# The first tiles' last decays taken out ahead of their flags, in an attention and two-expert-block kernel

## The chip, the core and the metric

The kernel runs on one core of a Trainium2 chip. The metric is the device time of one execution in microseconds (us), as the median of several runs. The kernel before takes 728.8 us (three runs: 727.46, 728.80 and 737.34).

## What is computed

Three stages follow each other on 3072 tokens of width 384 (4 sequences of 768 tokens, 8 heads of 48). The first is a linear attention with a decaying state, step by step:

```
for t in range(S):
    cur = einsum('bhd,bhe->bhde', u * k_t, v_t)
    y[t] = einsum('bhd,bhde->bhe', r_t, state + cur)
    state = w_t[..., None] * state + einsum('bhd,bhe->bhde', k_t, v_t)
```

The second sends each token to one of 8 experts (argmax of `x @ w_gate + bias`), computes `relu(x @ w1[e]) @ w2[e]` and scales by the softmax weight of that expert. The third is a dense block, `max(x @ v1, x @ v2, x @ v3) @ v_out`.

## The kernel before, in words

The attention works on 24 tiles of 128 tokens, 6 to a sequence, all heads at once. The rest of the kernel (experts and dense block, matmuls of 128x256 and 128x512) isn't touched. For each tile two blocks come from memory: `tq`, the transposed r, k and decay w (`load_t`, one DMA of 576 KB, into one of four buffers; tile 0's comes in three pieces, w first), and `nat`, the rows of v, r and k (`load_n`, 608 KB). All of these loads are issued by SyncE (SP), in the order of the program. Each load fills 96 of the 128 partitions of `tq`; the rest is padding, written once at the start by `pads(j)` for each buffer j (zeros for r and k, ones for w), and a load can't be issued before its buffer's padding is written.

What a tile goes through, by function, and on which engine:

- `flags(i)` (ScalarE): two passes over the tile's decays, 128x512, that sum how far they lie outside of allowed bounds into `flag`. Nothing reads `flag` before the plan for the experts (`check_w`).
- `cut_w(i)` (ScalarE): copies each head pair's last decay (128x4) into `wl`, and overwrites it in `tq` by a multiplication with `keep` (0 or 1 by partition). `flags` reads the decays whole, so it stands ahead of `cut_w`.
- `scan_f(i)` (VectorE): the running product of the decays into `prod`, by a scan over 128x512 that needs the cut decays; then a reciprocal, and `pt`, the product with `wl`.
- `mul_r`, `scan_r`, `mul_k` (VectorE): r times the product, the reverse scan, and k times it: `rt` and `kt`.
- `ktrans(i)`, `scores(i)` (TensorE): transposes of `kt`, copied to `kn` by ScalarE, and the 128x128 products of `kt` and `rt`, copied to `am` by ScalarE (two copies) and masked by GpSimd (POOL, `affine_select`).
- `kv(i)`, `output(i)` (TensorE): the tile's addition to the state, and the output into `yb` from `am`, v and the state `sbd`.
- `uterm_a(i)` (POOL), `usum(i)` (VectorE), `uterm_b(i)` (POOL): the term with u, from `nat`; `output_x(i)` (VectorE) adds it to `yb` and gives x, which `columns(i)` transposes (TensorE), ScalarE copies, and `logits_of` uses.

No scheduler decides the order: it is as written, and each engine runs its instructions strictly in that order. Tiles 0 and 1 stand in a prologue of their own; from then on the loop at `for i in range(NTILE - 2)` runs `scan_f` of tile i+2 together with the matmuls of tiles i and i+1, and `flags` and `cut_w` of tile i+3. `rows()` is a generator that puts some constants for the routing between the work of tiles 1 to 3: on VectorE a cast `mf`, which TensorE transposes (L172), and on POOL some twenty small memsets and iotas. `warm(n)` issues n matmuls of 128x512 on a tile of zeros, `wide`, whose result nobody reads; `WARM` lists how many stand at each of its places, and the fourth entry, for ordinary tiles of the loop, is 0.

Of the kernel before, what the change touches and what calls it, by code (L numbers as in the profile page):

```python
# [9 lines left out]
F32 = mybir.dt.float32  # L10
F32R = mybir.dt.float32r
BF16 = mybir.dt.bfloat16
I32 = mybir.dt.int32
U32 = mybir.dt.uint32
ACTF = mybir.ActivationFunctionType
# [6 lines left out]

W_LO, W_HI = 0.7, 1.4
P_LO = 1e-22
BIG = 1000000.0
OOB = 1 << 20
SLOT = object()
# [13 lines left out]


FIRST_GO = (9, 0, 0, 7, 8)
WARM = (16, 6, 4, 0, 3, 0)


@with_exitstack
def kernel(ctx: ExitStack, tc: tile.TileContext, rkw_t, v_t, vrk, u, modality, w_gate, bias, w1, w2, v1, v2,
# [56 lines left out]
    def ct(shape, dt, name):  # L105
        return const.tile(shape, dt, name=name)
# [18 lines left out]
    wg = ct([128, KD, E], F32, "wg")  # L125
    b0 = ct([128, 2, E], F32, "b0")
    brow = ct([128, NTILE, E], F32, "brow")
    flag = ct([128, NTILE, 2], F32, "flag")
    ctl = ct([128, 64], I32, "ctl")
    gctl = ct([128, 4], I32, "gctl")  # L130
    idxm = ct([128, NTILE], I32, "idxm")
# [541 lines left out]
    def attention(hooks):  # L673
        with ExitStack() as es:
# [26 lines left out]
            def v4(t):  # L701
                return t.rearrange("p (a c) -> p a c", a=HP)
# [6 lines left out]
            tq = [e1.tile([128, 3 * 512], F32, name=f"tq{j}") for j in range(NB)]  # L709
            keep = e1.tile([128, 1], F32, name="keep")  # L710
            DVE.memset(tq[0][96:128, 1024:1536], 1.0)
            DVE.memset(wide, 0.0)

            def r_of(i):
                return v4(tq[i % NB][:, 0:512])
# [4 lines left out]
            def w_of(i):  # L720
                return v4(tq[i % NB][:, 1024:1536])

            def pads(j, rk=POOL.memset, w=POOL.memset):
                rk(tq[j][:, 0:1024], 0.0)
                w(tq[j][:, 1024:1536], 1.0)

            def zeros(out, _):
                for q in range(2):
                    ACT.copy(out[:, q * 512:(q + 1) * 512], wide)
            POOL.memset(tq[0][96:128, 0:1024], 0.0)  # L730
            DVE.memset(tq[0][0:PAD, 1024:1536], 1.0)
            POOL.memset(neglo[:, 0:1], W_LO)
            POOL.memset(neglo[:, 1:2], -W_HI)
            POOL.memset(keep, 0.0)
            POOL.memset(keep[0:PAD], 1.0)
            POOL.memset(keep[96:128], 1.0)
            POOL.memset(keep[96:PAD + 2 * D], 0.0)
            DVE.memset(d1f, P_LO)
            DVE.memset(v4(d1f)[:, :, 0:1], 1.0)
            DVE.memset(d1r, 0.0)  # L740
            POOL.memset(tq[0][0:PAD, 0:1024], 0.0)
            pads(1, zeros)
            pads(2, DVE.memset, DVE.memset)
            make_identity(nc, ident)
            for t in sbd:
                POOL.memset(t, 0.0)
            pads(3)

            T = [dict() for _ in range(NTILE)]

            def load_t(i, parts=(slice(0, 3),)):
                b, c = divmod(i, NC)
                for q in parts:
                    SP.dma_start(out=tq[i % NB][PAD:PAD + 2 * D, q.start * 512:q.stop * 512],
                                 in_=rkw_t[b, c, :, :, q].rearrange("o d q a t -> (o d) (q a t)"))

            def load_n(i):
                n = np_.tile([128, HN + 2 * DM], F32, tag="nat", name="nat")
                SP.dma_start(out=n, in_=vrk[i * 128:(i + 1) * 128])
                T[i]["v"] = heads(n[:, 0:HN])[:, :, 0:D]  # L760
                T[i]["r"], T[i]["k"] = n[:, HN:HN + DM], n[:, HN + DM:HN + 2 * DM]
                T[i]["uv"] = n[:, HN:HN + DM]
# [19 lines left out]
            def flags(i):  # L782
# [4 lines left out]
                ACT.activation(out=jk, in_=wr, func=ACTF.Relu, scale=1.0, bias=neglo[:, 1:2],  # L787
                               accum_out=flag[:, i, 1:2])

            def cut_w(i):  # L790


                last = w_of(i)[:, :, 127:128]
                s = T[i]
                s["wl"] = a2.tile([128, HP, 1], F32, tag="wl", name="wl")
                ACT.copy(s["wl"], last)
                ACT.activation(out=last, in_=last, func=ACTF.Copy, scale=keep)

            def scan_f(i):

                s = T[i]
                f = tq[i % NB]
                DVE.tensor_tensor_scan(out=prod, data0=f[:, 1023:1535], data1=d1f, initial=0.0, op0=ALU.mult, op1=ALU.max)  # L803
                end = v4(prod)[:, :, 127:128]
                s["pt"] = a3.tile([128, HP, 1], F32, tag="pt", name="pt")
                DVE.reciprocal(v4(d1r)[:, :, 126:127], end)
                DVE.tensor_tensor(out=s["pt"], in0=end, in1=s["wl"], op=ALU.mult)

            def mul_r(i):
                s = T[i]  # L810
# [119 lines left out]
            loads, rows = constants_rest(pes)  # L930
            load_t(0, [slice(q, q + 1) for q in (2, 0, 1)])
            load_t(1)
            load_n(0)
            load_u()
            load_t(2)
            load_n(1)
            loads()
            SP.dma_start(out=wg, in_=w_gate.rearrange("(k p) e -> p k e", p=128))
            load_n(2)
            warm(WARM[0])  # L940
            flags(0)
            for i in range(2):
                cut_w(i)
                scan_f(i)
                mul_r(i)
                scan_r(i)
                mul_k(i)
                if i == 0:
                    flags(1)
                    ktrans(0)  # L950
                    scores(0)
                    warm(WARM[1])
                uterm_a(i)
            load_t(3)
            load_t(4)
            flags(2)
            cut_w(2)
            for i in range(NTILE - 2):
                n = i + 2
                if i + 5 < NTILE:  # L960
# [9 lines left out]
                    output_x(i - 1)  # L970
                ktrans(i + 1)
                scores(i + 1)
                if i:
                    columns(i - 1)
                uterm_a(n)
# [13 lines left out]
                state_b(i)  # L989
                slot()  # L990
                slot()
                for j in (0, 1) if i == 0 else (i + 1,):
                    usum(j)
                    uterm_b(j)
                slot()
# [621 lines left out]
```

## Time and profile before

| | |
|---|---|
| median of three runs | 728.8 us |
| the profiled execution | 736.0 us, span from first to last instruction 734.2 us |
| mean granted TensorE clock, share of 2.4 GHz | 0.973 |
| TensorE matmuls busy | 698.3 us, 95% of the span |
| VectorE busy | 468.8 us, 64% |
| ScalarE busy | 321.8 us, 44% |
| POOL busy | 327.6 us, 45% |

The attention fills the first quarter of the span, the experts and the dense block the rest. The shares are means over stages that differ: in the start, which the change is about, the engines wait for each other and for loads, and the clock that was granted to TensorE falls to half of 2.4 GHz and comes back. In a timeline row the first number is the start, the second the time during which the row's instructions ran (an "x2" row merges two); what stands in brackets is how long the engine had been idle just before, and what ended that.

### The profile page before, as it was taken

To read this page: it belongs to the slowest core of one execution; us is meant where nothing else is said; L and a number is where in the kernel's file an instruction comes from. 1 tells how busy PE (TensorE), PEld (TensorE's weight loads), DVE (VectorE), ACT (ScalarE), POOL (GpSimd) and SP (SyncE) were. 2 spreads that over 40 slices of the span, in tenths; PEclk is the share of its full clock that TensorE was granted. 3 is DMA by queue.
4 is the path that set the end of the run, shared out by engine and by line. 5 is a ranking of instruction groups with operands and counts; after the bars stand their busy time and mean duration, and the time that the engine had idled before them with its cause. 6 is when DMAs were issued, how large, how long until landed. Compare 5 with 4: busy or idle time off the path is not lost.

```text
span 734.2 us, 13120 instructions
## 1 busy us (share of the span) xinstructions
PE 698.3 (95%) x4948; PEld 636.8 (87%) x4956; DVE 468.8 (64%) x858; ACT 321.8 (44%) x695; POOL 327.6 (45%) x386
## 2 busy tenths in 40 slices
PE   5999999998799999999999999999999999999996
PEld 2788878897799899999999987988988989889886
DVE  5888988888387988889897979524234143142330
ACT  5576757674213656666666633221212212112111
POOL 5676669697546767777674435010200201101002
PEclk9799999998799989999999999999999999999999
DMA  8877769961023222222254232020200200000001
GB/s 239 224 224 218 230 179 246 283 219 35 1 75 109 66 87 66 65 83 71 66 164 151 87 130 87 1 86 1 76 11 1 89 0 12 33 0 33 12 0 48
DMA packets 28509, 69.86 MB, mean 95 GB/s; under 512 B 5173, under 2 KB 15189, under 8 KB 28436
## 3 DMA queue, kind: packets, MB, share of 16 engines
q1 hardware_dynamic: 23636, 59.43, 27.5%
q0 software_dynamic: 4800, 9.49, 4.1%
q8 instruction: 41, 0.67, 0.4%
q14 instruction: 32, 0.26, 0.1%
HBM read 83.24 MB, written 14.38 MB: 133 GB/s over the span
## 4 chain that ended last, share of the span: by engine, by line
PE 39%; issue 36%; DVE 11%; POOL 6%; ACT 4%; DMA 2%; another core or an unknown queue 1%; POOLq 0%; SPq 0%; DVEq 0%; ACTq 0%
PE mm L1226 9%; PE mm L1227 9%; PE mm L1225 9%; POOL out_dram L1310 3%; PE yb L867 3%; PE mm L833 2%; DMA nat<-in_vrk_dram 2%; PE lgps L222 1%; DVE prod L803 1%; PE yb L873 1%; PE lgps L855 1%; PE tp L846 1%; PE tp L1214 1%; ACT am L836 1%
## 5 line engine op out<-in xcount | busy, mean ns | idle before, releaser
L1290 DVE TENSOR_TENSOR w2r<-mm,w2r 128x512 f32<-128x512 f32 x72 | 49.7, 690 | 145.7 <-PE mm L1227 145.6
L1310 POOL DMA_INDIRECT out_dram<-w2r,oi_all x24 | 26.0, 1083 | 244.9 <-ACT w2r L1309 244.3
L1225 PE MATMUL mm<-w1h,vh 128*128 128x512 f32 x324 | 126.3, 390 | 1.5 <-DVE w2r L1290 1.5
L1226 PE MATMUL mm<-w1l,vh 128*128 128x512 f32 x324 | 126.2, 389 | 0.0
L1227 PE MATMUL mm<-w1h,vl 128*128 128x512 f32 x324 | 126.1, 389 | 0.0
L1226 PE MATMUL mm<-hl,w2h 128*128 128x256 f32 x312 | 91.0, 292 | 3.3 <-DVE hl L1239 3.3
L1225 PE MATMUL mm<-hh,w2h 128*128 128x256 f32 x312 | 91.7, 294 | 1.5 <-issue 1.5
L1227 PE MATMUL mm<-hh,w2l 128*128 128x256 f32 x312 | 90.7, 291 | 0.0
L1225 PE MATMUL mm<-xh,w1h 128*128 128x256 f32 x306 | 87.7, 287 | 0.0
L1227 PE MATMUL mm<-xh,w1l 128*128 128x256 f32 x306 | 87.4, 286 | 0.0
L1226 PE MATMUL mm<-xl,w1h 128*128 128x256 f32 x306 | 87.4, 286 | 0.0
L1292 ACT CAST w2h<-w2r 128x512 fp32r<-128x512 f32 x36 | 22.4, 622 | 135.8 <-DVE w2r L1290 135.8
L1225 PEld LDWEIGHTS mm<-w1h,vh 128*128 128x128 f32 x324 | 60.8, 188 | 14.9 <-DVE w2r L1290 2.4
L1227 PEld LDWEIGHTS mm<-w1h,vl 128*128 128x128 f32 x324 | 60.8, 188 | 12.7
L1226 PEld LDWEIGHTS mm<-w1l,vh 128*128 128x128 f32 x324 | 60.8, 188 | 12.4
L580 POOL TENSOR_TENSOR w2l<-w2r,w2h 128x384 fp32r<-128x384 f32 x44 | 50.8, 1158 | 37.9 <-ACT w2h L578 33.3
L1226 PEld LDWEIGHTS mm<-hl,w2h 128*128 128x128 f32 x312 | 62.3, 200 | 4.4 <-DVE hl L1239 4.0
L1225 PEld LDWEIGHTS mm<-hh,w2h 128*128 128x128 f32 x312 | 62.4, 200 | 1.8 <-issue 1.8
L1227 PEld LDWEIGHTS mm<-hh,w2l 128*128 128x128 f32 x312 | 62.2, 199 | 0.0
L1225 PEld LDWEIGHTS mm<-xh,w1h 128*128 128x128 f32 x306 | 59.6, 195 | 0.0
L1226 PEld LDWEIGHTS mm<-xl,w1h 128*128 128x128 f32 x306 | 59.6, 195 | 0.0
L1227 PEld LDWEIGHTS mm<-xh,w1l 128*128 128x128 f32 x306 | 59.6, 195 | 0.0
(294 smaller groups left out, 1614.9 us busy)
## 6 DMA issues: line engine op xcount, KB each, us to landing
w1r<-in_moe_w_dram SPq DMA_DIRECT2D x10, 1536.0 KB
w2r<-in_moe_w_dram SPq DMA_DIRECT2D x10, 1536.0 KB
nat<-in_vrk_dram SPq DMA_DIRECT2D x24, 608.0 KB
tq<-in_rkw_t_dram SPq DMA_DIRECT2D x23, 576.0 KB
stg<-in_moe_w_dram SPq DMA_DIRECT2D x18, 384.0 KB
x2t<-raw SPq DMA_DIRECT2D x12, 384.0 KB
w1r<-x2t SPq DMA_DIRECT2D x12, 384.0 KB
xs<-x SPq DMA_DIRECT2D x23, 192.0 KB
```

Of the source, the lines that this page charges most:

```text
L222: PE.matmul(logits[:, t, :], lhsT=xT[:, kk, :], rhs=wg[:, kk, :], start=(kk == 0), stop=(kk == KD - 1))
L580: eng.tensor_tensor(out=lo, in0=src, in1=hi.bitcast(F32), op=ALU.subtract)
L803: DVE.tensor_tensor_scan(out=prod, data0=f[:, 1023:1535], data1=d1f, initial=0.0, op0=ALU.mult, op1=ALU.max)
L833: PE.matmul(ps[o][:, p * 128:(p + 1) * 128], lhsT=s["kt"][q, p, :], rhs=s["rt"][q, p, :], start=True, stop=True)
L836: ACT.copy(am[:, 4 * o:4 * o + 4, :], ps[o].rearrange("p (h t) -> p h t", h=4))
L867: PE.matmul(yb[:, h * DV:(h + 1) * DV], lhsT=s["am"][:, 4 * (h % 2) + h // 2, :], rhs=s["v"][:, h, :], start=(h == 0), stop=(first and h = ...
L1225: PE.matmul(oc, lhsT=wh[:, kk, sl], rhs=xh[:, kk, :], start=first and kk == 0, stop=False)
L1226: PE.matmul(oc, lhsT=wh[:, kk, sl], rhs=xl[:, kk, :], start=False, stop=False)
L1227: PE.matmul(oc, lhsT=wl[:, kk, sl], rhs=xh[:, kk, :], start=False, stop=last and kk == nk - 1)
L1290: DVE.tensor_tensor(out=hv, in0=o, in1=hv, op=ALU.max)
L1292: ACT.copy(self.h2h[:, c, :], hv)
L1310: ins = POOL.indirect_dma_start(out=out[:, :], out_offset=bass.IndirectOffsetOnAxis(ap=ids[q][:, 0:1], axis=0), in_=ob, in_offset=None, bo ...
```

## The change

1. In the prologue and for tile 2, `cut_w` comes first and a new function `flags_behind` takes the place of `flags` behind it: it flags 127 of 128 decays of each head pair in `tq`, and the last one from `wl`, so four passes instead of two. `flag` gets three more columns for it.
2. The prologue no longer has `ktrans(0)` and `scores(0)` between tiles 0 and 1: they follow both tiles' `mul_k`. `cut_w(2)` follows them, and `flags_behind(2)` and `uterm_a(1)` move into the loop behind `scores(1)`. `usum(1)` and `uterm_b(1)` move from the loop's first pass into its second.
3. The padding of buffer 1 is written by VectorE (r, k) and POOL (w) right at the start, that of buffer 2 by ScalarE (r, k) and POOL (w); buffer 3's comes ahead of the memsets of `sbd`. `wide` is zeroed behind buffer 1's padding.
4. SP loads `tq` of tile 2 ahead of `nat` of tile 0, and `tq` of tile 3 ahead of `nat` of tile 2.
5. The prologue's `warm` calls have 20 and 4 matmuls instead of 16 and 6.
6. `pt` is computed with a lower bound of 1e-10 on `wl`, by one `scalar_tensor_tensor` instead of a `tensor_tensor`.

```diff
+WL_LO = 1e-10
-WARM = (16, 6, 4, 0, 3, 0)
+WARM = (20, 4, 4, 0, 3, 0)
-    flag = ct([128, NTILE, 2], F32, "flag")
+    FIRST = 3
+    flag = ct([128, NTILE + FIRST, 2], F32, "flag")
...
             DVE.memset(tq[0][96:128, 1024:1536], 1.0)
-            DVE.memset(wide, 0.0)
+            POOL.memset(tq[0][96:128, 0:1024], 0.0)
...
-            POOL.memset(tq[0][96:128, 0:1024], 0.0)
+            pads(1, DVE.memset)
+            DVE.memset(wide, 0.0)
             DVE.memset(tq[0][0:PAD, 1024:1536], 1.0)
+            POOL.memset(tq[0][0:PAD, 0:1024], 0.0)
+            DVE.memset(d1f, P_LO)
+            DVE.memset(v4(d1f)[:, :, 0:1], 1.0)
+            DVE.memset(d1r, 0.0)
             POOL.memset(neglo[:, 0:1], W_LO)
...
-            DVE.memset(d1f, P_LO)
-            DVE.memset(v4(d1f)[:, :, 0:1], 1.0)
-            DVE.memset(d1r, 0.0)
-            POOL.memset(tq[0][0:PAD, 0:1024], 0.0)
-            pads(1, zeros)
-            pads(2, DVE.memset, DVE.memset)
+            pads(2, zeros)
             make_identity(nc, ident)
+            pads(3)
             for t in sbd:
                 POOL.memset(t, 0.0)
-            pads(3)
...
+            def flags_behind(i):
+                jk = a1.tile([128, 512], BF16, tag="jk", name="jk")
+                for q, sign in enumerate((-1.0, 1.0)):
+                    ACT.activation(out=v4(jk)[:, :, 0:127], in_=w_of(i)[:, :, 0:127], func=ACTF.Relu, scale=sign,
+                                   bias=neglo[:, q:q + 1], accum_out=flag[:, i, q:q + 1])
+                    ACT.activation(out=v4(jk)[:, :, 127], in_=T[i]["wl"][:, :, 0], func=ACTF.Relu, scale=sign,
+                                   bias=neglo[:, q:q + 1], accum_out=flag[:, NTILE + i, q:q + 1])
...
-                DVE.tensor_tensor(out=s["pt"], in0=end, in1=s["wl"], op=ALU.mult)
+                DVE.scalar_tensor_tensor(out=s["pt"], in0=s["wl"], scalar=WL_LO, in1=end, op0=ALU.max, op1=ALU.mult)
...
             load_t(1)
+            load_t(2)
             load_n(0)
             load_u()
-            load_t(2)
             load_n(1)
+            load_t(3)
             loads()
...
             warm(WARM[0])
-            flags(0)
             for i in range(2):
                 cut_w(i)
                 scan_f(i)
+                flags_behind(i)
                 mul_r(i)
                 scan_r(i)
                 mul_k(i)
-                if i == 0:
-                    flags(1)
-                    ktrans(0)
-                    scores(0)
-                    warm(WARM[1])
-                uterm_a(i)
-            load_t(3)
+            ktrans(0)
+            scores(0)
+            uterm_a(0)
+            warm(WARM[1])
+            cut_w(2)
             load_t(4)
-            flags(2)
-            cut_w(2)
             for i in range(NTILE - 2):
...
                 scores(i + 1)
+                if i == 0:
+                    flags_behind(2)
+                    uterm_a(1)
...
-                for j in (0, 1) if i == 0 else (i + 1,):
+                for j in ((0,), (1, 2))[i] if i < 2 else (i + 1,):
                     usum(j)
                     uterm_b(j)
```

How the order on the engines changes is shown at three places. The first is ScalarE's prologue, before (`jk` is a pass of `flags`, `wl` and the write into `tq` are `cut_w`, `kn` and `am` the copies of tile 0's matmuls):

```order
L785 ACTIVATE jk_228,flag_89<-tq0_160,neglo_110 128x512
L787 ACTIVATE jk_228,flag_89<-tq0_160,neglo_110 128x512
L796 COPY wl_231<-tq0_160 128x4
L797 ACTIVATE tq0_160<-tq0_160,keep_164 128x4
L785 ACTIVATE jk_244,flag_89<-tq1_161,neglo_110 128x512
L787 ACTIVATE jk_244,flag_89<-tq1_161,neglo_110 128x512
L848 COPY kn_252<-tp_247 128x512
L836 COPY am_254<-mm_255 128x512
L836 COPY am_254<-mm_256 128x512
L796 COPY wl_278<-tq1_161 128x4
L797 ACTIVATE tq1_161<-tq1_161,keep_164 128x4
```

Tile 1's cut stood behind the copies of tile 0's transposes and scores. In the changed kernel the same place reads:

```order
L807 COPY wl_233<-tq0_160 128x4
L808 ACTIVATE tq0_160<-tq0_160,keep_164 128x4
L796 ACTIVATE jk_240,flag_89<-tq0_160,neglo_110 128x4x127
L798 ACTIVATE jk_240,flag_89<-wl_233,neglo_110 128x4
L796 ACTIVATE jk_240,flag_89<-tq0_160,neglo_110 128x4x127
L798 ACTIVATE jk_240,flag_89<-wl_233,neglo_110 128x4
L807 COPY wl_251<-tq1_161 128x4
L808 ACTIVATE tq1_161<-tq1_161,keep_164 128x4
L796 ACTIVATE jk_258,flag_89<-tq1_161,neglo_110 128x4x127
```

Each tile's cut stands ahead of its flags, and tile 1's has moved ahead of every copy from TensorE. The second place is ScalarE at tile 3, in the loop's first pass, in the changed kernel (before, the four rows of `flags_behind(2)`, `jk_339`, were not there, and the rest stood in the same order):

```order
L847 COPY am_324<-mm_326 128x512
L796 ACTIVATE jk_339,flag_89<-tq2_162,neglo_110 128x4x127
L798 ACTIVATE jk_339,flag_89<-wl_298,neglo_110 128x4
L796 ACTIVATE jk_339,flag_89<-tq2_162,neglo_110 128x4x127
L798 ACTIVATE jk_339,flag_89<-wl_298,neglo_110 128x4
L787 ACTIVATE jk_365,flag_89<-tq3_163,neglo_110 128x512
L789 ACTIVATE jk_365,flag_89<-tq3_163,neglo_110 128x512
L807 COPY wl_368<-tq3_163 128x4
L808 ACTIVATE tq3_163<-tq3_163,keep_164 128x4
```

Tile 2's flags now stand between tile 1's `am` copies and tile 3's cut. The third place is POOL in the loop's first two passes; `nat` with `u_b` is `uterm_a`, `nat` with `sh` is `uterm_b`, and nat_200, 204, 209 are tiles 0, 1, 2. Before:

```order
L770 TENSOR_TENSOR nat_209<-nat_209,u_b_156 128x384
L771 TENSOR_TENSOR nat_209<-nat_209 128x384
L780 TENSOR_TENSOR nat_200<-nat_200,sh_368 128x384
L780 TENSOR_TENSOR nat_204<-nat_204,sh_371 128x384
L166 MEMSET zt_390 128x384
L174 MEMSET on_394 128x128
L837 AFFINE_SELECT am_408<-am_408 128x512 x2
```

In the changed kernel tile 1's `uterm_b` (nat_204 with `sh_485`) comes behind the second pass's masks, tile 3's `uterm_a` and the routing constants, the last of which are the first three rows here:

```order
L203 MEMSET oe_105 128x4
L206 MEMSET d0c3_83 128x32
L207 MEMSET d0c3_83 128x8
L782 TENSOR_TENSOR nat_204<-nat_204,sh_485 128x384
L782 TENSOR_TENSOR nat_210<-nat_210,sh_488 128x384
L206 MEMSET d0c8_84 128x72
```

It moved by one pass of the loop; tile 2's (nat_210) stayed where it was, right behind.

## Rows read from the trace of the kernel before

**Rows 1.** Busy time by stretch: TensorE, weights, VectorE, ScalarE, POOL; granted clock, DMA share, GB/s

```profile
6.00:28.00 22.00, 14.51 (x87) 10.01 (x85) 15.70 (x29) 10.30 (x30) 10.07 (x14) 0.71 1.01 270
11.90:15.30 3.40, 3.40 (x21) 2.08 (x21) 0.03 (x1) 2.09 (x6) 0.96 (x2) 0.50 1.03 270
15.30:18.70 3.40, 1.20 (x19) 0.65 (x17) 3.30 (x6) 1.79 (x6) 3.24 (x5) 1.00 1.05 304
18.70:28.90 10.20, 8.97 (x55) 7.27 (x56) 8.90 (x18) 4.17 (x11) 6.20 (x9) 0.50 0.94 237
```

**Rows 2.** Timeline of ScalarE in the prologue

```profile
4.43 0.72 ACT L785 ACTIVATE jk<-tq,neglo 128x512 bf16<-128x512 f32 x1 [1.16 <-POOL ident masks.py:199]
...
6.06 0.18 ACT L796 COPY wl<-tq 128x4 f32<-128x4 f32 x1
6.33 0.30 ACT L797 ACTIVATE tq<-tq,keep 128x4 f32<-128x4 f32 x1
9.38 0.72 ACT L785 ACTIVATE jk<-tq,neglo 128x512 bf16<-128x512 f32 x1 [2.75 <-DMA tq<-in_rkw_t_dram]
...
11.82 0.59 ACT L848 COPY kn<-tp 128x512 f32<-128x512 f32 x1 [0.78 <-PE tp L846]
13.68 1.07 ACT L836 COPY am<-mm 128x512 f32<-128x512 f32 x2 [1.27 <-PE mm L833]
```

**Rows 3.** Timeline of VectorE: memsets, the scans of tiles 0 to 5, one cast

```profile
3.88 0.91 DVE L724 MEMSET tq<- 128x1024 f32 x1 [0.20 <-issue]
4.85 0.48 DVE L725 MEMSET tq<- 128x512 f32 x1
6.72 1.23 DVE L803 TENSOR_TENSOR_SCAN prod<-tq,d1f 128x512 f32<-128x512 f32 x1 [1.38 <-ACT tq L797]
...
15.27 1.23 DVE L803 TENSOR_TENSOR_SCAN prod<-tq,d1f 128x512 f32<-128x512 f32 x1 [4.26 <-ACT tq L797]
...
19.66 1.23 DVE L803 TENSOR_TENSOR_SCAN prod<-tq,d1f 128x512 f32<-128x512 f32 x1
...
25.92 1.23 DVE L803 TENSOR_TENSOR_SCAN prod<-tq,d1f 128x512 f32<-128x512 f32 x1 [0.71 <-ACT tq L797]
...
27.33 0.29 DVE L164 CAST mf<-mi 24x128 f32<-24x128 int32 x1
...
34.64 1.23 DVE L803 TENSOR_TENSOR_SCAN prod<-tq,d1f 128x512 f32<-128x512 f32 x1 [1.60 <-ACT tq L797]
...
40.72 1.23 DVE L803 TENSOR_TENSOR_SCAN prod<-tq,d1f 128x512 f32<-128x512 f32 x1 [0.61 <-ACT tq L797]
```

**Rows 4.** Timeline of TensorE: first warm-up, transposes, outputs, scores of tile 2

```profile
1.94 5.16 PE L926 MATMUL tp<-wide 128*128 128x512 bf16 x16 [1.94 <-DVE wide L712]
11.16 0.63 PE L846 MATMUL tp<-ident,kt 128*128 128x128 f32 x4 [4.06 <-DVE kt L824]
...
22.74 3.65 PE L867 MATMUL yb<-nat,am 128*128 128x48 f32 x16
...
29.80 1.16 PE L833 MATMUL mm<-rt,kt 64*128 64x128 f32 x16
...
31.27 1.88 PE L867 MATMUL yb<-nat,am 128*128 128x48 f32 x16
```

**Rows 5.** DMA issues of the attention's blocks, size of each

```profile
nat<-in_vrk_dram SPq DMA_DIRECT2D x24, 608.0 KB
tq<-in_rkw_t_dram SPq DMA_DIRECT2D x23, 576.0 KB
```

**Rows 6.** Groups on VectorE, 85 to 260 us: busy us, mean ns

```profile
L807 DVE TENSOR_TENSOR pt<-prod,wl 128x4 f32<-128x4 f32 x12 | 1.8, 152 | 0.0
...
L447 DVE SCALAR_TENSOR_TENSOR gb<-gexp,pids 128x4 f32<-128x4 f32 x1 | 0.2, 152 | 0.0
```

**Rows 7.** Timeline of POOL, second pass of the loop

```profile
31.70 1.23 POOL L837 TENSOR_SCALAR_AFFINE_SELECT am<-am 128x512 f32<-128x512 f32 x2 [2.87 <-ACT am L836]
...
37.39 0.83 POOL L780 TENSOR_TENSOR nat<-nat,sh 128x384 f32<-128x384 f32 x1
```

## The prediction, made before the changed kernel ran

> **What bounds the kernel now.** I read the timelines of the four engines over the first 45 us beside each other, since nothing behind the attention is edited, then the windows for the granted clock and the DMA share. In the timelines the reader is to see what each `scan_f` waited for: it starts a tile's work on VectorE, and its starts are the ruler of this prediction. They stand at 6.72, 15.27, 19.66, 25.92, 34.64 and 40.72 us for tiles 0 to 5 [rows 3]. Only tile 2's follows its predecessor at once, after 4.39 us, which is VectorE's own time for a tile; all others waited for ScalarE's cut of the decays. The longest wait, 4.26 us at tile 1, isn't a load: ScalarE had tile 1's block at 9.38 us, but in its order the copies of tile 0's transposes and scores come first, the last from 13.68 us on [rows 2]. TensorE in turn was idle for 4.06 us before tile 0's transposes [rows 4]; its granted clock was 0.50 from 11.9 to 15.3 us and, after 3.4 us in which it was busy for 1.20, again from 18.7 to 28.9 us [rows 1]. The output of a tile took 3.65 us at that clock and 1.88 us at the full one, a factor of 1.94 [rows 4]. Loads are the other limit: from 6 to 28 us the DMA engines were busy throughout, at 270 GB/s [rows 1].
>
> **The change, step by step, as shifts of the scans.**
>
> *Tile 0.* ScalarE's flags ran from 4.43 us to 6.06 us; from there cut and scan start are 0.66 us apart [rows 2, 3]. With the cut first, the scan starts at 4.43 + 0.66 = 5.09 us: 1.63 us earlier. The memsets it could wait for are covered: VectorE's list ended at 5.33 us, and its last one, 0.48 us, goes to POOL, so it ends before 4.9.
>
> *Tile 1.* VectorE is free of tile 0 at 5.09 + 4.39 = 9.48 us. The block was there at 9.38; cut and start add 0.66: 10.04 us instead of 15.27, 5.2 us earlier. The load may land earlier, since its buffer no longer waits for ScalarE's zeros; VectorE then is the floor, 9.48. I take 10.04: the engines of the DMA were already full.
>
> *Tile 2.* VectorE is free at 10.04 + 4.39 = 14.43. ScalarE does its cut of tile 1 until 10.0; then `flags_behind(1)`: two long passes, 1.63 us, and two short ones, each at least the 0.30 us of a 128x4 pass [rows 2] and at most as long as the long ones (1.63 together), so 2.2 to 3.3 us. They are nearest to the former, with a read of the accumulator each; I take 2.4, until 12.4. The copies (0.59 and 1.07 us, rows 2), whose matmuls are done by then, bring it to 14.1, the cut to 14.7: scan at 14.7 instead of 19.66, 5.0 us earlier. The first warm-up, 16 matmuls in 5.16 us, begins later by one memset of 0.91 us and has four more; it ends near kt(0), at 9.5 us, and delays no one by more than tenths.
>
> *Tile 3.* Here part is given back. kt(1) is ready at 10.04 + 4.39 = 14.4; transposes 0.63 and scores 1.16 us [rows 4] end at 16.2 at the full clock, the copies at 17.3. Then `flags_behind(2)` stands in the way (19.7), then `flags(3)` (21.3) and cut and start: 22.0 instead of 25.92, 3.9 us earlier. Its load: behind 9.38 us come two blocks of 576 and two of 608 KB and u's 192 KB, 2.62 MB [rows 5], at 270 GB/s 9.7 us: 19.1, just in time for 19.7. Later loads are in the order and amount of before, and needed some microseconds after they land; they cost nothing unless DMA slows to the 237 GB/s of 18.7 to 28.9 us [rows 1], which would cost 0.7 us here.
>
> *Tile 4.* In TensorE's order the transpose of the cast `mf` stands ahead of tile 2's transposes, and VectorE makes that cast 1.41 us behind tile 3's scan [rows 3]: 22.0 + 1.4 + 0.2 = 23.6. TensorE is done with output(0) (1.88 us from 16.2) and the short work behind it (four warm matmuls at 0.3 us each, the state's products) by about 19.8, so it idles for 3.8 us. Idle stretches like this one took the clock to half twice before [rows 1, 4], so I expect half clock for tile 2's transposes and scores: 1.79 x 1.94 = 3.5 us, until 27.3 (full clock: 25.6). From the end of these scores to the next scan it was 34.64 - 30.96 = 3.7 us [rows 3, 4]: the scan is at 31.0 (29.3), against 34.64. VectorE alone allows 22.0 + 7.1 + 0.5 for the second `usum` = 29.6, where 7.1 is 34.64 - 25.92 less 1.60 idle. So 3.6 us earlier (5.0 at full clock).
>
> *Tile 5.* `uterm_b(1)` now stands behind POOL's masks, `uterm_a(3)` and the routing constants. That chain ended 38.22 - 30.96 = 7.3 us behind tile 2's scores [rows 4, 7]: at 34.6 (32.9). x of tile 1 needs it some 2 us behind tile 4's scan (the place of the cast in tile 3, 1.4, and a product of 128x512), at 33.0 (31.6), so x comes 1.3 to 1.6 us late, and what follows from x (columns, copy, flags, cut) sets tile 5's scan. This leaves 2.0 us (3.6 at full clock) of the gain.
>
> From there both kernels do the same work in the same order, at some 6 us a tile (40.72 - 34.64), and I know of nothing that gives the shift back. `pt` as a `scalar_tensor_tensor` costs nothing: both forms took 152 ns at 128x4 [rows 6]. The passes of flags that come on top stand where ScalarE had idle time, but for tile 2's, which is counted. The two warm matmuls less behind tile 0 are covered by TensorE's wait for kn.
>
> **Sum.** Between 2.0 and 3.6 us less, nearer to the first: 2.5. The profiled execution took 736.0 us, so 733.5 in its terms; it is 7.2 us above the median of 728.8, so I predict 728.8 - 2.5 = 726.3, in round numbers 726 us.
>
> The Trainium skill, page "TensorE: Matmul & The Clock Gate", section "HAM oscillation — how this bites in real kernels", speaks against the change at tile 4: it says that a kernel whose TensorE idles too long between bursts falls back to the half clock and begins each burst slow. The trace agrees as far as its two falls go. By this rule the sum is the 2.0; without it, 3.6.
>
> **Rivals.**
>
> *More stays.* The clock holds through the idle time, or the constants on POOL run earlier than I think, and the shift of tiles 2 and 4, 5 us, remains: 723.5. For it: the clock was kept from 15.3 to 18.7 us while TensorE was busy for only 1.20, so it doesn't fall at once [rows 1]. Against it: 3.8 us of idle time. Chance 0.20.
>
> *Slower: the half clock stays.* If the clock falls at tile 2 and the tile's own matmuls can't bring it back, no warm matmuls follow until tile 5's end (the entry for ordinary tiles is 0). A tile takes 6.1 us with TensorE nearly full, so at 1.94 it takes 11.8: 5.7 us lost per tile. One tile more gives 726.3 + 5.7 = 732, four tiles 749, and it decides the sign from the first. For it: from 18.7 to 28.9 us the clock stayed at half although TensorE was busy for 8.97 of 10.2 us with a tile's transposes, scores and output [rows 1]. Against it: from 11.9 us on, scores with warm matmuls behind them brought it back within 3.4 us. Chance 0.12, of which 0.04 for more than three tiles.
>
> The Trainium skill, in the same page's section "What's actually happening", says that the default is the throttled state and that activity releases it; by that a tile's matmuls alone should do it, which would make this rival cost at most a tile.
>
> *Nothing is left.* DMA runs at its limit up to 28 us in any case; if tile 3's and 4's blocks land 2 us later than I work out, or POOL's late `uterm_b(1)` costs 4 rather than 1.5, the time is 728 to 730. For it: 19.1 against 19.7 is a thin margin. Chance 0.20.
>
> My forecast, 724.5 to 727.5, has 0.45. The last 0.03 is for more than 8 us less, by a stretch of half clock elsewhere that falls away.
>
> **Range and chances.** The runs of before lie 10 us apart (727.46 to 737.34) for the same program, and a median of three can fall in either part, so every case carries an upward tail of some 8 us. The range is 717 to 736: below it is the gain of over 9 us, above it the rival of several slow tiles, or the forecast in the upper part with a tile lost. About 2% (14.6 us) is what a measurement of this kernel can tell from no change. Faster than 714.2 none of the cases gives but for a part of the last, 0.03. Slower than 743.4 is the slow rival with over three tiles, 0.04. The rest, 0.93, is no change.
>
> **What would show it.** Each step: scans at 5.1, 10.0, 14.7, 22.0, 31.0 (29.3 to 29.6 with the clock kept) and about 38.7 us. VectorE's wait before tile 1's scan below 1 us. ScalarE's four passes at tile 2 between the `am` copies and `flags(3)`, 2.4 us. TensorE idle for some 4 us before the transpose of `mf`, and a granted clock of 0.50 behind it. POOL's `uterm_b(1)` as what x of tile 1 waited for. The prediction is wrong if tile 1's scan still waits for ScalarE's copies, if tile 3's block lands behind 20 us, if the shift at tile 5 isn't that at tile 20, or if the clock stays at half beyond tile 2.

## The result, and the profile after

The change made the kernel slower: 739.18 us (median of 20 runs, 730.08 to 751.93) against 732.57 us (20 runs, 726.94 to 741.0) for the kernel before, run beside it; the ratio is 1.0081, with an interval of 1.0053 to 1.011, so 4 to 8 us more. I had predicted 726. The runs of one kernel lie up to 22 us apart with the clock that TensorE was granted; the ratios here and below are of comparable runs, and the profiled execution of the changed kernel, 742.05 us (span 740.2), is from the upper part.

Two things happened, and I had foreseen one of them. First the start, as one profiled execution of either kernel shows it; how far executions of one and the same start differ is told further down. This is VectorE's timeline of the changed kernel, the scans of tiles 0 to 6, to be held against [rows 3] (6.72, 15.27, 19.66, 25.92, 34.64, 40.72 us; tile 6 stood at 47.15):

```profile
7.66 1.23 DVE L814 TENSOR_TENSOR_SCAN prod<-tq,d1f 128x512 f32<-128x512 f32 x1 [2.90 <-DMA tq<-in_rkw_t_dram]
...
12.04 1.23 DVE L814 TENSOR_TENSOR_SCAN prod<-tq,d1f 128x512 f32<-128x512 f32 x1
...
16.54 1.23 DVE L814 TENSOR_TENSOR_SCAN prod<-tq,d1f 128x512 f32<-128x512 f32 x1 [0.20 <-ACT tq L808]
...
23.89 1.23 DVE L814 TENSOR_TENSOR_SCAN prod<-tq,d1f 128x512 f32<-128x512 f32 x1 [2.27 <-ACT tq L808]
25.30 0.67 DVE L166 CAST mf<-mi 24x128 f32<-24x128 int32 x1
...
32.99 1.23 DVE L814 TENSOR_TENSOR_SCAN prod<-tq,d1f 128x512 f32<-128x512 f32 x1 [2.33 <-ACT tq L808]
36.60 0.56 DVE L904 TENSOR_TENSOR x<-yb,nat 128x384 f32<-128x384 f32 x1 [1.53 <-POOL nat L782]
...
40.48 1.23 DVE L814 TENSOR_TENSOR_SCAN prod<-tq,d1f 128x512 f32<-128x512 f32 x1 [0.41 <-ACT tq L808]
...
50.01 1.23 DVE L814 TENSOR_TENSOR_SCAN prod<-tq,d1f 128x512 f32<-128x512 f32 x1 [4.06 <-ACT tq L808]
```

The wait of tile 1 for ScalarE's copies is gone, as predicted, and tile 1 is 3.2 us earlier. But tile 0 is 0.9 us later, for a load, and the gain shrinks from tile to tile: 3.2, 3.1, 2.0, 1.7, 0.2 us, then 2.9 us lost. ScalarE's timeline answers to [rows 2]: the cut now ends at 5.0 us instead of 6.6, and tile 0's scan could have followed it.

```profile
4.71 0.30 ACT L808 ACTIVATE tq<-tq,keep 128x4 f32<-128x4 f32 x1
...
10.15 0.30 ACT L808 ACTIVATE tq<-tq,keep 128x4 f32<-128x4 f32 x1
...
18.66 1.07 ACT L847 COPY am<-mm 128x512 f32<-128x512 f32 x2 [0.50 <-PE mm L844]
19.62 0.73 ACT L796 ACTIVATE jk<-tq,neglo 128x508 bf16<-128x508 f32 x1
...
21.78 0.72 ACT L787 ACTIVATE jk<-tq,neglo 128x512 bf16<-128x512 f32 x1
...
23.56 0.30 ACT L808 ACTIVATE tq<-tq,keep 128x4 f32<-128x4 f32 x1
```

TensorE's and POOL's timelines ([rows 4], [rows 7]) show where the rest went: TensorE waits 4.01 us for the mask's cast `mf`, as predicted, and later 1.77 us for x of tile 1, which waits for POOL's `uterm_b(1)`:

```profile
26.02 0.24 PE L174 MATMUL lgps<-ident,mf 24*128 24x24 f32 x1 [4.01 <-DVE mf L166]
...
27.23 2.08 PE L844 MATMUL mm<-rt,kt 64*128 64x128 f32 x16
...
37.30 0.52 PE L911 MATMUL tp<-ident,x 128*128 128x128 f32 x3 [1.77 <-DVE x L904]
```

```profile
35.74 1.62 POOL L782 TENSOR_TENSOR nat<-nat,sh 128x384 f32<-128x384 f32 x2
```

Behind either wait the granted clock is at half of 2.4 GHz, as the windows show (columns as in [rows 1]):

```profile
26.20:29.60 3.40, 3.40 (x23) 2.85 (x23) 3.37 (x9) 0.79 (x2) 0.00 (x0) 0.50 1.00 297
29.60:39.80 10.20, 8.43 (x92) 7.95 (x91) 6.27 (x14) 7.40 (x18) 9.35 (x31) 1.00 0.51 154
39.80:46.70 6.90, 6.90 (x52) 6.08 (x50) 5.67 (x12) 2.08 (x8) 2.04 (x3) 0.51 0.85 254
```

The second thing lies 400 us further on, in the dense block, whose code is the same. These rows are the dense block's 324 matmuls with weights `vh` and moving rows `w1h`: min, median and max duration in ns, then the first and last start. Before:

```profile
L1225 PE MATMUL mm<-w1h,vh x324: 387/389/504, 429.5 to 714.1; 128*128 128x512 f32 x162
```

After:

```profile
L1236 PE MATMUL mm<-w1h,vh x324: 392/395/501, 431.0 to 720.6; 128*128 128x512 f32 x162
```

The block begins 1.5 us later than before, and takes 289.6 instead of 284.6 us from the first of these starts to the last. Of the two executions' difference of 6.0 us, 5.0 arose here, at full clock in both. There are three such groups of 324 (`w1h` with `vh`, `w1l` with `vh`, `w1h` with `vl`), and in all three a matmul takes 395 to 396 ns instead of 389 to 390; from one start to the next it is 233 ns instead of 227. 972 times 6 ns is 5.8 us.

What ties these matmuls to the change is memory. `flag` has 27 x 2 columns instead of 24 x 2, 216 bytes in a partition instead of 192. Tiles on the left side of SBUF are placed one behind the other in steps of 32 bytes, so all that come behind `flag` lie 32 bytes further, the dense weights `vh` and `vl` among them (24032 became 24064); the moving rows `w1h` and `w1l`, on the right side, stayed at 157664 and 169952. In the kernel before, the weights and the moving rows all lie at 480 modulo 512 bytes. These places are those of the program's allocation; no trace shows an address, and what the runs can show is what a shift does. That gave the theory: the pace of these matmuls depends on where their operands lie. Its rival: the slower block is a consequence of the start, in clock or in loads, and the address an accident.

### The profile page after: what moved, and what is told of

The parts are those of the page before. It is cut to its first block, busy times and chain, and to the rows that moved or that the text cites. A ratio compares the mean times of both kernels' runs of the same rounds, so it can differ in the third digit from the quotient of the medians.

```text
span 740.2 us, 13134 instructions
## 1 busy us (share of the span) xinstructions
PE 706.5 (95%) x4950; PEld 640.5 (87%) x4958; DVE 466.6 (63%) x857; ACT 323.4 (44%) x707; POOL 329.3 (44%) x387
## 4 chain that ended last, share of the span: by engine, by line
issue 36%; PE 35%; DVE 12%; POOL 7%; ACT 3%; DMA 2%; POOLq 0%; DVEq 0%; ACTq 0%
PE mm L1237 8%; PE mm L1238 8%; PE mm L1236 7%; POOL out_dram L1321 3%; PE yb L878 3%; PE mm L844 2%; PE lgps L224 2%; DMA order<-idg,places 1%; PE yb L884 1%; DVE w1l L582 1%; PE lgps L866 1%; PE tp L857 1%; PE tp L911 1%; PE tp L1225 1%; DVE ya L614 1%
## 5 line engine op out<-in xcount | busy, mean ns | idle before, releaser
L1236 PE MATMUL mm<-w1h,vh 128*128 128x512 f32 x324 | 128.2, 396 | 0.9 <-DVE w2r L1301 0.9
L1238 PE MATMUL mm<-w1h,vl 128*128 128x512 f32 x324 | 128.2, 396 | 0.0
L1237 PE MATMUL mm<-w1l,vh 128*128 128x512 f32 x324 | 128.1, 395 | 0.0
L1237 PE MATMUL mm<-hl,w2h 128*128 128x256 f32 x312 | 89.3, 286 | 2.1 <-DVE hl L1250 2.1
L1236 PE MATMUL mm<-hh,w2h 128*128 128x256 f32 x312 | 90.1, 289 | 0.0
L1238 PE MATMUL mm<-hh,w2l 128*128 128x256 f32 x312 | 89.0, 285 | 0.0
L1238 PEld LDWEIGHTS mm<-w1h,vl 128*128 128x128 f32 x324 | 60.9, 188 | 14.7
L1237 PEld LDWEIGHTS mm<-hl,w2h 128*128 128x128 f32 x312 | 60.6, 194 | 2.5 <-DVE hl L1250 2.5
L1236 PEld LDWEIGHTS mm<-hh,w2h 128*128 128x128 f32 x312 | 60.7, 195 | 0.0
L1238 PEld LDWEIGHTS mm<-hh,w2l 128*128 128x128 f32 x312 | 60.6, 194 | 0.0
```

The costliest lines, as they stand in the source:

```text
L1236: PE.matmul(oc, lhsT=wh[:, kk, sl], rhs=xh[:, kk, :], start=first and kk == 0, stop=False)
L1237: PE.matmul(oc, lhsT=wh[:, kk, sl], rhs=xl[:, kk, :], start=False, stop=False)
L1238: PE.matmul(oc, lhsT=wl[:, kk, sl], rhs=xh[:, kk, :], start=False, stop=last and kk == nk - 1)
```

## Experiments

**The shift alone.** The kernel before, once with `flag` widened, which moves everything on the left by 32 bytes (b_flag32), once with an unused tile of 32 bytes ahead of `vh`, which moves the dense block's weights and staging tiles only (b_w32).

```diff
-    flag = ct([128, NTILE, 2], F32, "flag")
+    flag = ct([128, NTILE + 3, 2], F32, "flag")
...
-        DVE.tensor_reduce(out=fl, in_=flag, axis=AX.XY, op=ALU.max)
+        DVE.tensor_reduce(out=fl, in_=flag[:, 0:NTILE], axis=AX.XY, op=ALU.max)
```

> The kernel before with nothing changed but the size of flag (27 columns instead of 24, the new ones unread), so that every tile that is allocated behind it, the dense block's split weights vh and vl among them, lies 32 bytes further on. Theory A (the place of the dense block's weights in SBUF sets the pace of its 972 matmuls of 128x512): their mean rises from 389 to about 395 ns, start to start from 227 to 233 ns, and the time by 972 x 6 ns = 5.8 us, 0.8%. Theory B (the added time is made in the prologue and by the clock that falls behind it, and the 6 ns belong to that execution): no change, 389 ns.

```diff
         wres = pool(ctx, "wres", 1)
+        wres.tile([128, 8], F32, name="gap32")
```

> The kernel before with an unused tile of 32 bytes ahead of the dense block's weights alone: the attention's tiles lie where they lay. Theory A: again 395 ns and +5.8 us. If it is the attention's tiles whose place matters: no change. Theory B: no change.

Measured: 740.34 us, ratio 1.0106 (1.0051 to 1.0161), and 737.71 us, ratio 1.0089 (1.005 to 1.0128), beside 729.84 us for the kernel before. With not one instruction of the start changed, the whole loss is there. The second kernel's row, over a block of 291.1 us:

```profile
L1225 PE MATMUL mm<-w1h,vh x324: 388/395/499, 422.5 to 713.6; 128*128 128x512 f32 x162
```

**A shift by 64 bytes.** The changed kernel with 32 columns in `flag`, alone (a_64) and with `usum` and `uterm_b` of tile 1 back in the loop's first pass (a_64_pool).

```diff
-    flag = ct([128, NTILE + FIRST, 2], F32, "flag")
+    flag = ct([128, NTILE + 8, 2], F32, "flag")
...
-        DVE.tensor_reduce(out=fl, in_=flag, axis=AX.XY, op=ALU.max)
+        DVE.tensor_reduce(out=fl, in_=flag[:, 0:NTILE + FIRST], axis=AX.XY, op=ALU.max)
```

> The changed kernel with flag at 32 columns, so that the tiles behind it lie 64 bytes further on than before instead of 32, and stand to the 64-byte grid as before. Theory A: 389 ns again, and 5.8 us less than the changed kernel: between -2.5 us (the forecast for the prologue) and +0.5 us against before. Theory B: 395 ns or not, the time stays some 6 us above before.

The second has, besides:

```diff
-                for j in ((0,), (1, 2))[i] if i < 2 else (i + 1,):
+                for j in (0, 1) if i == 0 else (i + 1,):
```

> As a_64, with the sum and product of tile 1's u term (usum(1), uterm_b(1)) back in the loop's first pass, ahead of the routing constants on POOL. If x of tile 1 waits for POOL's late product (1.5 us in the trace) and TensorE's pause behind it lets the clock fall: tile 1's x about 1.5 us earlier, no stretch of half clock near 40 us, scans of tiles 5 and 6 earlier by 2 and 4 us, and 2 to 4 us less than a_64. If not: as a_64.

Measured: 744.03 us, ratio 1.0109 (1.0045 to 1.0173), and 731.42 us, ratio 1.003 (0.9992 to 1.0068). The matmuls stayed at 233 ns, so a grid of 64 bytes is not it; that form of the theory fell. That POOL's product in its old place is worth several us is what the two ratios suggest, but their intervals overlap, and the profiles don't show it: x of tile 1 no longer waits for POOL in a_64_pool, yet tile 6's scan stands at 54.84 us against 54.13 in a_64, because in both the clock was at half for 27.3 us, from 25.0 and from 24.3 us on. The scans 2 and 4 us earlier that I expected were not there.

**Which places are slow.** One kernel with gaps between the weights (b_gaps), one with weights and moving rows shifted alike (b_both32).

```diff
-        vh = [wres.tile([128, KD, F2], F32R, name=f"vh{i}") for i in range(3)]
-        vl = [wres.tile([128, KD, F2], F32R, name=f"vl{i}") for i in range(3)]
+        vh, vl = [], []
+        for part, to, gaps in (("h", vh, (16, 16, 32)), ("l", vl, (80, 16, 32))):
+            for i, n in enumerate(gaps):
+                wres.tile([128, n], F32, name=f"gap{part}{i}")
+                to.append(wres.tile([128, KD, F2], F32R, name=f"v{part}{i}"))
```

> The kernel before; unused tiles between the second expert's weights set their places apart: vh0 and vl0 lie 64 bytes beyond the kernel before's place, counted modulo 512 bytes, vh1 and vl1 128 bytes, vh2 and vl2 256 bytes, the output weights 256 bytes. If the pace of a matmul hangs on the weights' place modulo 64 bytes, all three groups keep 227 ns from start to start; modulo 128 bytes, vh0 goes at 233 ns and vh1 and vh2 at 227; modulo 256 bytes, vh0 and vh1 at 233 and vh2 at 227; if only the very residue of the kernel before (480 modulo 512, the same as that of the moving rows) is fast, all three go at 233 ns, and the time is about 735 us (5.8 us more). If the address has nothing to do with it and the 32-byte shift slowed the block by something else, all stay at 227 ns and the time at about 729 us.

The other is the first experiment's kernel with one more tile, the last on the right side:

```diff
             self.hl = p.tile([128, KF, TW], F32R, name="hl")
+            p.tile([128, 120], F32, name="gapr")
```

> The kernel before, with flag 27 columns wide as in the first experiment (everything on the left of SBUF 32 bytes further), and an unused tile of 480 bytes behind hl on the right side, so that the moving rows w1h, w1l and all on that side also lie 32 bytes further modulo 512. If what counts is that weights and moving rows have the same place modulo 512, the 972 matmuls go at 227 ns again (m1 mean 389 to 390 ns) and the run is near the kernel before, 727 to 733 us. If the weights' own place counts, they stay at 233 ns (395 ns), and the time near 737 to 740 us.

Measured, in one run each: 737.37 us with the gaps, 726.73 us with both sides shifted (729.09 us for the kernel before). The gaps:

```profile
L1225 PE MATMUL mm<-w1h,vh x324: 388/395/502, 427.2 to 715.9; 128*128 128x512 f32 x162
```

Both sides shifted by 32 bytes:

```profile
L1226 PE MATMUL mm<-w1h,vh x324: 387/389/499, 420.6 to 705.0; 128*128 128x512 f32 x162
```

The second is the decisive one. The weights lie where they lay in the slow kernel, at 0 modulo 512, and the matmuls are quick, since the moving rows lie there too: 284.4 us for the block. It is not the weights' own place but that of the two operands to each other. With the gaps, the mean from start to start, worked out from the matmuls' starts, is about 233 ns at a distance of 64 bytes, 232 at 128 and 230 at 256, where one of three groups (`w1l` with `vh`) goes at 226. So of the distances tried only 0 modulo 512 is fully quick; 256 is between.

**The change with the old distance.** `flag` with 88 columns moves the left side by 512 bytes in all. Once alone (a_512), once with POOL's products back as in a_64_pool (a_512_pool).

```diff
-    flag = ct([128, NTILE + FIRST, 2], F32, "flag")
+    flag = ct([128, NTILE + 64, 2], F32, "flag")
...
-        DVE.tensor_reduce(out=fl, in_=flag, axis=AX.XY, op=ALU.max)
+        DVE.tensor_reduce(out=fl, in_=flag[:, 0:NTILE + FIRST], axis=AX.XY, op=ALU.max)
```

> The changed kernel, with flag 88 columns wide (the reduction over its first 27 as in the change), so that everything on the left lies 512 bytes further than before the change, and the weights have the kernel before's place modulo 512. If the place of the dense weights is what made the change slow, their 972 matmuls go at 227 ns again, 5.8 us come off, and what is left is the prologue's own balance in the profile of the change (first output row 1.6 us late): ratio to the kernel before about 0.997 to 1.003. If the loss has another cause, the ratio stays at 1.008.

> a_512, and tile 1's and tile 2's products on POOL issued as in the kernel before (both of tiles 0 and 1 in the first pass). If the late product on POOL at 35.7 us, the wait of PE behind it and the lost clock (39.8 to 46.7 us) cost about 3 us or more, the scan of tile 6 starts 3 us or more earlier than in a_512 and the ratio is about 0.993 to 0.997, a gain. If the product's place is worth nothing, the ratio is that of a_512.

Measured: 734.67 us, ratio 1.0031 (0.9986 to 1.0076), and 731.7 us, ratio 1.0007 (0.9972 to 1.0043). The block of a_512 takes 284.1 us:

```profile
L1236 PE MATMUL mm<-w1h,vh x324: 387/389/501, 420.7 to 704.8; 128*128 128x512 f32 x162
```

So the block's loss is gone, and nothing measurable is left of the change, to either side: a_512's runs go from 725.8 to 749.2 us. The ratio alone would not show this, since its interval reaches into that of the change (1.0053 to 1.011); the block's time does. My expectation of a gain for a_512_pool was not met; in its profile the clock was at half from 23.5 to 40.5 us.

**Where the start's gain goes.** Three edits to a_512: the order of tile 0's pieces (a_512_k), 12 warming matmuls in TensorE's wait for `mf` (a_512_warm), and tile 3's cut ahead of its flags (a_512_cut).

```diff
-            load_t(0, [slice(q, q + 1) for q in (2, 0, 1)])
+            load_t(0, [slice(q, q + 1) for q in (2, 1, 0)])
```

> a_512 with tile 0's pieces loaded in the order decays, k, r instead of decays, r, k. If the first scan waits for k's piece (its run over the whole tile begins at k's last column), it starts at about 5.1 us, when tile 0's last decays are cut out, instead of 6.9 (k's last packet at 6.8); the product with r then waits for r's piece to about 6.8, and the scans of tiles 1 and 2 come about 1.5 us earlier, near 9.8 and 14.2 us. If the scan waits for the cut of the decays or for the flags behind it, nothing moves. The time itself: tile 3's scan waits for ScalarE's flags of tile 2 (1.8 us in a_512), which also come 1.5 us earlier, so 1 to 1.5 us at the end if the clock falls as in a_512, ratio about 0.998 to 1.002 within the scatter of the clock.

```diff
                 state_b(i)
+                if i == 0:
+                    warm(12)
```

> a_512 with 12 of the program's warming matmuls (128x512 bf16, 0.26 us each at full clock, about 3.1 us) on TensorE behind tile 0's state, in the 3.7 us in which it waits for the mask's cast (21.1 to 24.8 us). If that idle stretch is what lets the clock fall to half behind it (22.6 to 29.5 us in a_512's profile), the stretch behind it stays at full clock, the scan of tile 4 comes 1.5 to 3 us earlier (near 29 to 30 us instead of 31.8), and the runs gather at the quick end: ratio 0.994 to 0.998. If the clock falls anyway there, or further on whatever PE does here, the ratio stays at 1.000 to 1.004.

```diff
-                    flags_behind(2)
                     uterm_a(1)
...
-                    flags(i + 3)
+                    if i:
+                        flags(i + 3)
                     cut_w(i + 3)
...
                 state_b(i)
+                if i == 0:
+                    flags_behind(2)
+                    flags_behind(3)
```

> a_512 in which tile 3's last decays, too, are taken out in front of its flags, and the flags of tiles 2 and 3 stand on ScalarE behind tile 0's state. If ScalarE's six flag passes (18.4 to 22.1 us) are what tile 3's scan waits for, that scan starts near 20.9 us (end of DVE's sums of tile 0) instead of 22.7, and the mask's cast and TensorE's next work come 1.8 us earlier: idle before the mask's transpose about 1.9 us instead of 3.7, a smaller or no stretch at half clock behind it, scan of tile 4 at 28 to 30 us. If the data of tile 3 or TensorE hold the scan, it stays at 22.7.

Measured (735.29 us for the kernel before): 738.58 us, ratio 1.0014 (0.9982 to 1.0047); 739.84 us, ratio 1.0034 (0.999 to 1.0079); one run of 734.29 us. By themselves none is shown to help the time, and the 0.994 to 0.998 that I expected of the warming matmuls was missed; each does to its wait what its theory said. With k second, tile 0's scan, in VectorE's timeline:

```profile
5.04 1.23 DVE L814 TENSOR_TENSOR_SCAN prod<-tq,d1f 128x512 f32<-128x512 f32 x1 [0.29 <-ACT tq L808]
...
10.17 1.23 DVE L814 TENSOR_TENSOR_SCAN prod<-tq,d1f 128x512 f32<-128x512 f32 x1 [0.83 <-ACT tq L808]
```

This is the start that I had predicted, 5.1 and 10.0 us. But in the same execution, of 746.88 us, x of tile 1 waited for POOL and TensorE for x, and the clock then stayed at half for 27.3 us (TensorE's row, then the window):

```profile
36.66 0.52 PE L911 MATMUL tp<-ident,x 128*128 128x128 f32 x3 [2.43 <-DVE x L904]
```

```profile
38.90:66.20 27.30, 27.30 (x169) 25.42 (x168) 16.56 (x33) 10.75 (x30) 10.23 (x13) 0.50 0.52 161
```

With the warming matmuls the clock held through the mask's transpose, tile 2's scores took 1.16 instead of 2.08 us, and the scan of tile 4 came at 30.1 us; then the same wait for POOL, and half clock from 36.9 to 43.7 us. TensorE's timeline:

```profile
18.83 3.83 PE L937 MATMUL tp<-wide 128*128 128x512 bf16 x15
...
24.48 0.24 PE L174 MATMUL lgps<-ident,mf 24*128 24x24 f32 x1 [1.22 <-DVE mf L166]
...
25.24 1.16 PE L844 MATMUL mm<-rt,kt 64*128 64x128 f32 x16
...
34.39 0.52 PE L911 MATMUL tp<-ident,x 128*128 128x128 f32 x3 [1.92 <-DVE x L904]
```

With tile 3's cut in front, the scan of tile 3 came at 21.15 us without a wait, and TensorE's wait for `mf` was 1.46 us; the clock was at half nevertheless, from 24.2 to 37.9 us.

**All together** (a_512_best), with POOL's products in their old place and 6 warming matmuls instead of 12.

> The three together with the place of POOL's products as before the change (a_512_pool): k's piece second, flags of tiles 2 and 3 behind tile 0's state, 6 warming matmuls in what is left of TensorE's idle time. Expected from the parts: scans of tiles 1 to 4 near 9.8, 14.2, 19.4 to 20, 26.5 to 28 us against 15.3, 19.7, 25.9, 34.6 in the kernel before; if the rest of the attention keeps that, the end is 4 to 6 us earlier than the kernel before's quick runs: ratio 0.992 to 0.995. If the clock is lost later instead (a thin stretch further on), half of it goes: 0.996 to 1.000.

Measured: 731.63 us against 735.29, ratio 0.9951 (0.9913 to 0.9988): 1 to 6 us faster than the kernel before, at the edge of what I expected. The scans of tiles 0, 1, 3, 4 and 6 in the profiled execution, of 727.79 us, and the granted clock from 20 us on:

```profile
4.95 1.23 DVE L814 TENSOR_TENSOR_SCAN prod<-tq,d1f 128x512 f32<-128x512 f32 x1 [0.19 <-ACT tq L808]
...
10.20 1.23 DVE L814 TENSOR_TENSOR_SCAN prod<-tq,d1f 128x512 f32<-128x512 f32 x1 [0.79 <-ACT tq L808]
...
20.81 1.22 DVE L814 TENSOR_TENSOR_SCAN prod<-tq,d1f 128x512 f32<-128x512 f32 x1
...
28.13 1.23 DVE L814 TENSOR_TENSOR_SCAN prod<-tq,d1f 128x512 f32<-128x512 f32 x1 [0.27 <-ACT tq L808]
...
40.75 1.23 DVE L814 TENSOR_TENSOR_SCAN prod<-tq,d1f 128x512 f32<-128x512 f32 x1 [0.61 <-ACT tq L808]
```

```profile
20.00:90.80 70.80, 64.87 (x711) 58.76 (x712) 62.34 (x134) 52.11 (x141) 51.12 (x88) 1.00 0.81 238
```

No wait of TensorE between 16 and 60 us is longer than 1.38 us, the clock stays full to 90.8 us, and the scan of tile 6 stands at 40.75 us, 6.4 us earlier than in the profiled execution of the kernel before. The scans up to 144 us keep these 6.4 us. One execution is a poor ruler, though: with the start of the kernel before untouched, tile 6's scan stood at 45.34 us in b_both32, 46.11 in b_w32, 52.53 in b_gaps and 54.71 in b_flag32. Against the earliest of these a_512_best is 4.6 us ahead; a_512, at 45.95, and the changed kernel, at 50.01, lie within their spread.

## Why the prediction was wrong

**The step that failed** is "From there both kernels do the same work in the same order, [...] and I know of nothing that gives the shift back". The same work in the same order was true, and it took 5.0 us longer, because the change's new columns moved the weights of 972 matmuls by 32 bytes against the rows that they meet. I had read `flag` as a matter of ScalarE's passes and not of places. Of the 13 us between my 726 and the measured 739.18, 3.8 are the kernel before itself, 732.57 us here against the 728.8 of three runs that I started from; the ratio of 1.0081 is free of them. All five kernels with the weights off by 32 or 64 bytes take 289.6 to 291.2 us for the block, all eight with equal places 284.1 to 284.6 us (b_gaps, with mixed distances, 288.7). The Trainium skill, page "SBUF — State Buffer", section "Operand start alignment", asks only that an operand start at a multiple of its element's size, and is about what is permitted; 32 bytes meets it, and the trace shows 6 ns a matmul all the same.

**Tile 0** was mis-sized. The scan reads from k's last column on (`tq` is r, k, decays in a row, and the scan begins one element ahead of the decays), so it needs k's piece, which comes third. In the kernel before it had landed by 5.65 us, before flags and cut were through, and so no row showed it; in the changed one at 7.54 us. Instead of 5.09 the scan started at 7.66; a_512_k removes the wait. Why the piece came so late is not shown. The changed order has tile 1's block issued 1 us earlier (2.98 instead of 3.93 us) and tile 2's ahead of `nat`, and in all seven changed kernels that load k third it landed at 6.4 to 7.5 us; but with the loads of the kernel before it landed at 5.6 to 5.7 us in four kernels and at 7.25 in b_flag32, where tile 0's scan waited for it too, to 7.37. Most of the 2.6 us by which tile 0 came late runs through the chain: the later scans came 2.0, 1.8, 1.9, 2.0 and 1.8 us behind my 10.04, 14.7, 22.0, 31.0 and 38.7.

**Tiles 1 to 5** went as worked out but for that. ScalarE's passes for tile 2 stood between the `am` copies and `flags(3)` and took 2.1 us (2.4 predicted); tile 3's scan waited 2.27 us for them; TensorE idled 4.01 us (3.8) ahead of the mask's transpose; tile 2's scores ran at half clock, 2.08 us, and the clock was back behind them.

**POOL's late product** was named but priced too low. I counted 1.3 to 1.6 us of delay for tile 5; the trace shows 1.53. I had not counted a second stretch of half clock behind TensorE's wait for that x, 1.77 us: from 39.8 to 46.7 us, 3.1 us more at tile 6 (from 0.2 earlier to 2.9 later). It doesn't always follow: in a_512 x waited 1.52 us for POOL, TensorE idled for 1.28 ahead of x's transposes, and the clock stayed full from 29.5 to 90.9 us. The stretch is the rival "the half clock stays", at another place than I gave it. At its own place, at the wait for `mf`, it came about in a_64 and a_64_pool, with 27.3 us, where a tile took 11.3 us instead of 6.1; and with the start of the kernel before, in b_gaps and b_flag32, the clock was at half for 23.9 us behind the wait for tile 1. So my 10.2 us of half clock for that start [rows 1] were one execution's. In a_512_k it is there in full again, 27.3 us over the scans of three tiles: TensorE was busy all the time, and that did not bring the clock back sooner. The Trainium skill, page "TensorE: Matmul & The Clock Gate", section "What's actually happening", makes the clock follow how busy TensorE has been; the trace of a_512_k does not agree, with 27.30 us busy of 27.30 at half clock.

**What was right:** the wait at tile 1 was the order's and went; `pt` cost nothing (0.15 us, as [rows 6]); the warm-up and the memsets were covered; tile 3's load landed at some 19.3 us (19.1 predicted) and held nobody up. Two sums are off by tenths without consequence: 23.6 + 3.5 is 27.1 and not 27.3, and 728.8 - 5 is 723.8 and not 723.5.

Open is how much of the measured 4 to 8 us belongs to the start. The block accounts for 5.0 us in the profiles; the rest, and a_512's ratio, are within the scatter of the clock. Why 256 bytes of distance are half as bad stays open. In b_flag32 and b_w32 the block took some 1.5 us more than in the changed kernel with the same distance; most of it lies in the 432 matmuls of 128x384, 338 to 339 ns each against 335 to 336, and why is open as well.

## What to carry to other kernels

When a change adds or widens a tile, look at what it moves: the places of matmul operands that are allocated behind it can decide more than the edit, and the trace shows it as a shift in the mean duration of untouched matmuls. An idle wait of TensorE should be priced with the clock that may follow it, wherever it stands, and a part's gain is worth little while another wait a tile later still drops the clock: three edits that showed no gain alone were, together and with POOL's order restored, 0.5% faster than the kernel before. The starts of single executions should not be compared by a microsecond or two where the clock may fall: with the same code at the start tile 6's scan moved by 9 us. A wait that the trace of before doesn't show may have been covered by the very work that the change removes, so ask of each moved instruction which bytes it reads.

## What the runs showed of the hardware

- The dense block's matmuls of 128x512, with 4-byte operands and new weights for each, follow each other at 227 ns when weights and moving rows start at the same place modulo 512 bytes (by the program's allocation), and at 232 to 233 ns at distances of 32, 64 and 128 bytes. The weight loads' own rows do not move: 188 ns each before and after. The 128x384 matmuls of the same block, `voh` moving, took 334 to 335 ns in the kernel before, 335 to 336 in the changed one and 338 to 339 in b_flag32 and b_w32.
- The clock fell not only behind TensorE's long waits at the start (4.01 us in the changed kernel) but also behind single short ones between busy stretches: 1.46 us in a_512_cut, 1.77 us in the changed kernel, 1.92 us in a_512_warm, 2.43 us in a_512_k. It held behind 1.28 us in a_512 and 1.38 us in a_512_best. How long it stays down differs: 13.7, 6.9, 6.8 and 27.3 us behind these four waits, and 3.4 to 27.3 us with the waits of 2.8 to 4.3 us at the start.
- The landing of one small load among large ones varied by 2 us: tile 0's k, 192 KB, loaded third and issued at 2.45 us, landed at 5.65 us in the kernel before and at 7.25 in b_flag32 with the same loads behind it; with tile 1's block issued 1 us earlier it landed at 6.4 to 7.5 us in seven kernels.
